# Delta rule and expert attention on one core: a shorter norm for the first two units, a folded sign, and a re-planned order of steps

## The chip, the cores and the metric

The kernel runs on one core of one Trainium2 chip. The metric is device time in microseconds (us), of which lower is better: the median of three runs, for the kernel before 444.77 us (442.21 to 446.26). One per cent is 4.4 us. Names of engines: PE is TensorE (PEld its weight loads), DVE is VectorE, ACT is ScalarE, POOL is GpSimd, SP is SyncE, which only starts transfers here.

## The reference, cut to what matters

There are 4 batches, 8 heads, 768 tokens and a head width of 48. The first part is a delta rule over time for each head; its output, heads side by side (768 x 384 for each batch), is the input of the second part, an attention in four experts of which each token uses two.

```
k_n = k / (norm(k) + 1e-6)
for t in range(768):                       # per batch and head
    y[t]  = q[t] @ state
    state = state + beta[t] * outer(k_n[t], v[t] - k_n[t] @ state)
x = y, heads side by side                  # 4 x 768 x 384
logits = x @ w_gate; topk = the 2 largest of 4; w = softmax over these 2
for e in range(4):
    a   = causal softmax(0.125 * (x @ wq[e]) @ (x @ wk[e]).T)
    out += w[e] (0 where e is not chosen) * (a @ (x @ wv[e])) @ wo[e]
```

## The kernel before, in words

The work is cut into six units of 256 tokens, numbered n = 0 to 5: units 0, 1, 2 are the three thirds of one pair of batches, units 3, 4, 5 those of the other pair. A unit has four chunks c of 64 tokens, and every chunk has 16 pairs of batch and head. Within a chunk the recurrence is solved in closed form: products of keys (`ga`), a triangular system of the tokens among themselves, and then, chunk after chunk, the state.

The kernel is one long list of steps, the string `ORDER`. Each word is a step with its arguments (and, after an @, the PSUM banks that it uses): `s0.4` is row 4 of the first unit's solve. The list is walked once from left to right and every step writes its instructions at once, so the list sets the order of the work on every engine and of the transfers on SP. Engines wait for each other by semaphores only. No planner runs inside the kernel: the numbers and the order in the string are all there is.

The steps that matter here, for a unit n:

- `lk`, `lq`, `lt`, `lv`, `lc`, `ww` load from memory (SP). `ga` multiplies keys with keys on PE; `ge.n.c.0` and `ge.n.c.1` copy the products from PSUM on ACT (line 207, into gf and into at or ax). `dx` (ACT, line 397) and `dy` (DVE, line 402) put unit 0's products into another layout, and `bi` (DVE, line 442) transposes them into the matrix `B`, in which a partition holds one small triangular system. Unit 0's B is a part of the tile vs; the others use the tile b.
- `nm` makes the norms from the diagonal of B: `aa`, which is beta over the squared (norm + 1e-6), and `nt`, the norm + 1e-6, transposed. Units 0 and 1 use square roots on ACT, whose function table has to be loaded first; units 2 to 5 use Newton steps on DVE.
- For unit 0, `bz` (POOL, line 449) clears what lies above the diagonal, `bs` (DVE, line 454) scales B's rows with minus aa, and `s0.1` to `s0.15` (DVE, lines 459, 461, 468, 469) solve the system in 14 steps and scale the columns. For the other units `sv.n.0` (DVE, line 522), `sv.n.1` to `sv.n.31` (POOL, lines 528, 530, 532) and `sv.n.32` (DVE, line 536) do the same.
- `tn` and `bo` (DVE, lines 475 and 472) transpose back. `p1`, `w1`, `p2`, `w2`, `t2` join the halves of the systems for units 0 and 1, `m1`, `we`, `m2`, `me`, `tc0`, `cl` the blocks of 32 to 64.
- Then the recurrence, chunk by chunk: `vs` (POOL, line 586: values times nt), `ks`, `xs`, `tx` (PE: the transform), `us`, `ku`, `se`, `yy`, `yc`, `yh`, `yl`, and `hx`, six transfers on SP (line 674) that turn a part of the output (tile h) into the input of the second part (tile xu).
- The second part: `pj` (PE, xu with wh and wl: queries and keys), `kh`, `kl`, `pv`, `ve`, `lg`, `gt`, `mx`, `mk`, `mr`, `sc`, `ex`, `av`, `oe`, `ft`, `fo`, `oo`, `so`. `gp` and `pm` are the products of queries with keys for the first part and their masking (DVE, line 394).
- `fl.k` and `fz.k` are fillers: k matmuls on a tile of zeros (zb, bf16), 384 and 320 columns wide, whose results nobody reads.

Line 205 is the one helper that writes all matmuls, line 207 the one that writes most ACT copies, so matmuls and copies are told apart by their tiles.

Of the kernel before, what the change touches and what calls it, by code (L numbers as in the profile page):

```python
# [33 lines left out]
s0.7 lq.0.1 s0.8 ge.1.0.1 ge.1.0.0 s0.9 ax.0.1 fl.8@4 ga.1.2@23 lt.0.2 s0.10 s0.11 s0.12 ge.1.1.1 ax.0.0 fl.6@4
gp.0.3@56 s0.13 s0.14 s0.15 ge.1.2.1 ge.1.2.0 tn.0 wh.2 gd.1 lq.1.2 bo.0 fl.18@4 p1.0.0@7 lq.1.1 p1.0.1@2 w1.0.0.0 wh.1
w1.0.0.1 hold p1.0.3@3 w1.0.1.0 wl.2 pm.0.3.0 pm.0.3.1 p2.0.0@7 ww.4 wl.1 w1.0.1.1 lv.0.3 gp.0.1@56 w2.0.0 p2.0.1@4 ww.3
t2.0.0 bi.1 m1.0.0@7 w1.0.3.0 p1.0.2@2 we.0.0 tc0.0.0 pm.0.1.0 w1.0.2.0 cl.0.0.0 tc0.0.1 vs.0.0 w2.0.1 pm.0.1.1 cl.0.0.1
t2.0.1 fl.10@7 m2.0.0@67 m1.0.1@4 w1.0.2.1 me.0.0.0 vs.0.1 me.0.0.1 w1.0.3.1 tc0.1.0 tx.0.0@56 we.0.1 vs.0.3 nm.1.0
p2.0.2@4 us.0.0.0 cl.0.1.1 us.0.0.1 nm.1.1 ku.0.0 w2.0.2 yy.0.0@23 nm.1.2 se.0.0.1 yc.0.0 tc0.1.1 p2.0.3@7 se.0.0.0
sv.1.0 yh.0.0.1 yh.0.0.0 ks.0.1@56 sv.1.1 xs.0.1 sv.1.2 w2.0.3 yl.0.0.0 fl.5@4 m2.0.1@67 cl.0.1.0 yl.0.0.1 vs.0.2  # L40
me.0.1.1 me.0.1.0 wh.3 t2.0.2 fl.4@4 tx.0.1@67 t2.0.3 us.0.1.1 nm.1.3 wl.3 tc0.2.0 us.0.1.0 tc0.2.1 fl.6@4 yy.0.1@23
ww.5 sv.1.3 m1.0.2@6 lv.1.0 m1.0.3@4 sv.1.4 yc.0.1 we.0.3 wh.4 lq.1.3 ku.0.1 cl.0.2.0 yh.0.1.1 yh.0.1.0 gp.0.2@45 sv.1.5
se.0.1.1 yl.0.1.1 yl.0.1.0 we.0.2 sv.1.6 se.0.1.0 pm.0.2.0 hx.0.0 wl.4 pm.0.2.1 cl.0.2.1 fl.10@7 m2.0.2@56 sv.1.7
# [893 lines left out]
```

## Time and profile before

| | us |
|---|---|
| median of three runs (lowest, highest) | 444.77 (442.21, 446.26) |
| the profiled execution, whole | 444.41 |
| its span, first to last instruction | 442.7 |
| PE busy in the span | 412.6 (93%) |
| fillers (L205, p<-zb) among these | 39.7 |
| DVE, ACT, POOL busy | 272.3, 207.9, 209.7 |

The profile is of one execution, whose whole time is 1.71 us longer than its span and 0.36 us below the median. Times are counted from the start of the span. A matmul row counts as busy whether its result is used or not, so 93% holds the fillers too. Mean granted clock of TensorE over the span: 0.992 of full speed.

### The profile page before, as it was taken

The page shows a single profiled execution, that of the slowest core. Times are in us where ns is not written, and L with a number is a line of the kernel's source. Part 1 is how long each engine was busy: PE and PEld are TensorE (multiplying, and loading weights), DVE is VectorE, ACT ScalarE, POOL GpSimd, SP SyncE. Part 2 cuts the span into 40 slices and gives each one's busy share as a digit, 9 for nine tenths or more (in the row PEclk, how much of TensorE's full clock was granted, in tenths as well). Part 3 has the DMA queues.
Part 4 walks back from the last instruction along what each step waited for, and adds up shares of the span by engine and source line. Part 5 has one row for each costly group of instructions (what it writes and reads, how often), then busy time and mean ns, then how long its engine had stood idle before and what let it go on. Part 6 is the DMA issues. An engine that isn't in the chain of part 4 may idle for free.

```text
span 442.7 us, 22242 instructions
## 1 busy us (share of the span) xinstructions
PE 412.6 (93%) x10008; PEld 337.9 (76%) x10008; DVE 272.3 (62%) x557; ACT 207.9 (47%) x439; POOL 209.7 (47%) x407
## 2 busy tenths in 40 slices
...
GB/s 217 271 156 5 79 127 129 19 86 32 145 61 87 122 46 18 192 97 29 84 21 45 88 127 116 98 3 53 63 89 103 39 21 23 39 36 37 4 4 71
DMA packets 52895, 34.12 MB, mean 77 GB/s; under 512 B 34944, under 2 KB 46976, under 8 KB 52800
## 3 DMA queue, kind: packets, MB, share of 16 engines
...
q8 instruction: 78, 1.28, 1.3%
q14 instruction: 17, 0.14, 0.1%
...
## 4 chain that ended last, share of the span: by engine, by line
PE 58%; POOL 15%; DVE 12%; issue 6%; ACT 4%; DMA 3%; SPq 2%; DVEq 0%; ACTq 0%
PE p L205 57%; POOL b L530 7%; POOL tm L528 7%; SPq L674 2%; DMA xu<-h 2%; DVE qp L394 2%; PE p L840 1%; DVE gf L472 1%; DMA gf<-zb 1%; ACT gf L573 1%; DVE tn L475 1%; DVE z L609 1%; DVE b L522 1%; DVE mp L766 1%; DVE rr L430 1%
## 5 line engine op out<-in xcount | busy, mean ns | idle before, releaser
L528 POOL TENSOR_TENSOR tm<-b 128x30 f32<-128x30 f32 (+14 forms) x120 | 58.1, 485 | 41.6 <-DVE b L522 20.4
L530 POOL TENSOR_TENSOR b<-b,tm 128x30 f32<-128x30 f32 (+14 forms) x120 | 62.0, 517 | 9.4
L803 ACT ACTIVATE at<-p 128x768 f32<-128x768 f32 (+1 forms) x48 | 43.8, 919 | 33.3 <-PE p L205 31.9
L207 ACT ACTIVATE z<-p 48x384 f32<-48x384 f32 (+1 forms) x68 | 32.8, 483 | 34.7 <-DVE z L609 17.0
L766 DVE TENSOR_REDUCE mp<-p 128x2 f32<-128x1024 f32 (+3 forms) x40 | 44.3, 1115 | 6.2 <-PE p L205 5.4
L205 PE MATMUL p<-vs,at 128*64 128x65 f32 x1344 | 46.1, 224 | 0.6 <-issue 0.6
L205 PE MATMUL p<-xu,wh 128*128 128x512 f32 (+1 forms) x168 | 43.7, 386 | 2.6 <-DMA xu<-h 2.0
L394 DVE TENSOR_TENSOR qp<-p,cs 64x512 f32<-64x512 f32 x48 | 33.0, 687 | 21.1 <-PE p L205 20.4
L205 PEld LDWEIGHTS p<-vs,at 128*64 128x64 f32 x1344 | 42.0, 138 | 4.7 <-issue 1.9
L205 PE MATMUL p<-zb 128*128 128x384 bf16 (+1 forms) x204 | 39.7, 333 | 1.4 <-DVE e L337 1.2
L205 PEld LDWEIGHTS p<-xu,wh 128*128 128x128 f32 x168 | 28.2, 194 | 8.7 <-issue 2.1
L205 PE MATMUL p<-qp,z 64*48 64x64 f32 (+2 forms) x1120 | 30.6, 221 | 2.2 <-issue 0.9
L205 PE MATMUL p<-qh,kh 64*128 64x128 f32 (+1 forms) x192 | 30.3, 310 | 0.9 <-ACT at L803 0.6
L205 PEld LDWEIGHTS p<-qp,z 64*48 64x48 f32 (+2 forms) x1120 | 24.7, 120 | 7.8 <-DVE z L609 2.1
L807 POOL TENSOR_SCALAR_AFFINE_SELECT at<-at 128x512 f32<-128x512 f32 x24 | 16.3, 685 | 30.0 <-ACT at L803 30.0
L205 PEld LDWEIGHTS <-zb 128*128 128x128 bf16 x204 | 18.0, 100 | 12.5 <-issue 2.3
L586 POOL TENSOR_TENSOR kv<-kv,nt 128x384 f32<-128x384 f32 x24 | 19.7, 830 | 16.0 <-DVE nt L436 10.5
L205 PE MATMUL p<-qh,kl 64*128 64x128 f32 (+1 forms) x192 | 27.1, 277 | 0.0
L205 PE MATMUL p<-wh,xu 128*128 128x260 f32 x144 | 26.7, 296 | 0.4 <-DMA xu<-h 0.2
L205 PE MATMUL p<-ql,kh 64*128 64x128 f32 (+1 forms) x192 | 27.0, 276 | 0.0
L205 PE MATMUL p<-mr,sl 64*128 64x128 f32 (+1 forms) x192 | 26.9, 275 | 0.0
L760 DVE TENSOR_TENSOR p<-p,km 128x512 f32<-128x512 f32 (+1 forms) x32 | 18.0, 564 | 11.4 <-PE p L205 10.6
...
## 6 DMA issues: line engine op xcount, KB each, us to landing
...
```

The source lines that it names most:

```text
L205: T.matmul(o, lhsT=a, rhs=b, start=start, stop=True, skip_group_check=True)
L207: copy = lambda o, a: S.activation(o, a, AF.Copy)
L394: V.tensor_tensor(turns(QP[zi(n, c) % RQ][r, f]), gv(n, c)[r], PMK[r, None, None, :].to_broadcast([64, 2, 2, 128]), op=OP.mult)
L430: V.reciprocal(r, g0)
L528: G.tensor_tensor(tv, B2[:, i:i + 1, i + 1:].to_broadcast([128, i, m]), B2[:, 0:i, i:i + 1].to_broadcast([128, i, m]), op=OP.mult)
L530: G.tensor_tensor(B2[:, 0:i, i + 1:], B2[:, 0:i, i + 1:], tv, op=OP.add)
L586: G.tensor_tensor(vt, vt, NRM[n % 2][:, c * NP:c * NP + NP, None].to_broadcast([128, NP, HD]), op=OP.mult)
L674: nc.sync.dma_start(XU[n % 2][64 * f + HD:64 * f + 64, :, i, hb].bitcast(F32), H3[r:r + 16].bitcast(F32))
L760: V.tensor_tensor(g[:, :, :, 128 * nb - 128:], g[:, :, :, 128 * nb - 128:], KM[:, None, None, :].to_broadcast([128, 2, per, 128]), op=OP.add)
L766: V.tensor_reduce(o[:, :, y0:y0 + per], g, axis=AX.X, op=OP.max, negate=True)
L803: S.activation(at(n, b, y, kp)[:, :, 0:w], two(("sc", n, b, y, kp), w), AF.Exp, scale=0.125)
L807: G.affine_select(a, a, pattern=[[0, 2], [0, 2], [1, 128]], compare_op=OP.is_ge, fill=0.0, base=0, channel_multiplier=-1)
```

## The change: the norm of units 0 and 1, the scaling of unit 0, and a new order

**The norm of units 0 and 1.** Before, `nm.n.0` took two square roots on ACT, `nm.n.1` three DVE operations to make nn = norm + 1e-6, `nm.n.2` three more for aa, and `nm.n.3` the transposition. After, `nm.n.0` is one square root (of 4e-12 times x, for x the squared norm) and `nm.n.1` three DVE operations that make aa at once, from x + 2e-6 norm + 1e-12; `nm.n.2` takes the second square root and a copy of x on ACT, and `nm.n.3` makes the norm itself by one Newton step, adds 1e-6 and transposes, five DVE operations. **The first scaling.** `bs` multiplies with plus aa in one operation in place of two with minus aa; the solve of unit 0 subtracts where it added (`half`), and a new step `na` writes minus aa on ACT into unit 1's aa tile, for use in `s0.15`.

```diff
         if n < 2:
             if k == 0:
+                S.activation(nn, BD(n), AF.Sqrt, bias=E0, scale=4e-12)
+            elif k == 1:
+                V.scalar_tensor_tensor(nn, nn, 1e-12, BD(n), op0=OP.add, op1=OP.add)
+                V.reciprocal(r, nn)
+                V.tensor_tensor(aa, r, BT[:, n], op=OP.mult)
+            elif k == 2:
                 S.activation(g0, BD(n), AF.Sqrt, bias=E0)
-                S.activation(ss, BD(n), AF.Sqrt, bias=E0, scale=0.25)
-            elif k == 1:
+                copy(ss, BD(n))
+            else:
                 V.reciprocal(r, g0)
-                V.scalar_tensor_tensor(r, r, 0.5, BD(n), op0=OP.mult, op1=OP.mult)
-                V.scalar_tensor_tensor(nn, r, 1e-6, ss, op0=OP.add, op1=OP.add)
-            elif k == 2:
-                V.tensor_tensor(r, nn, nn, op=OP.mult)
-                V.reciprocal(r, r)
-                V.tensor_tensor(aa, r, BT[:, n], op=OP.mult)
-            else:
+                V.scalar_tensor_tensor(r, r, 0.5, ss, op0=OP.mult, op1=OP.mult)
+                V.tensor_scalar(r, r, 1e-6, None, op0=OP.add)
+                V.scalar_tensor_tensor(nn, g0, 0.5, r, op0=OP.mult, op1=OP.add)
                 V.transpose(nt, nn)
...
     def bs():
-        for x in range(2):
-            a, b = NV[0]["aa"][:, None, 16 * x:16 * x + 16].to_broadcast([128, 16, 16]), BX(0)[:, x]
-            V.scalar_tensor_tensor(b, b, -1.0, a, op0=OP.mult, op1=OP.mult)
+        a, b = NV[0]["aa"].rearrange("p (x i) -> p x i", x=2), BX(0)
+        V.tensor_tensor(b, b, a[:, :, None, :].to_broadcast([128, 2, 16, 16]), op=OP.mult)
+
+    def na():
+        S.activation(NV[1]["aa"], NV[0]["aa"], AF.Copy, scale=-1.0)
...
-        E.tensor_tensor(b[:, :, 0:i, i + 1:], b[:, :, 0:i, i + 1:], tv, op=OP.add)
+        E.tensor_tensor(b[:, :, 0:i, i + 1:], b[:, :, 0:i, i + 1:], tv, op=OP.add if n else OP.subtract)
...
-            a, b = NV[0]["aa"].rearrange("p (x i) -> p x i", x=2), BX(0)
+            a, b = NV[1]["aa"].rearrange("p (x i) -> p x i", x=2), BX(0)
```

**The order.** `ORDER` is written anew from its second line on. Two lines of it, around the first norm:

```diff
-lk.1.0 nm.0.1 lt.0.3 bz ci pm.0.0.1 lq.1.0 ge.0.2.1 ge.0.0.0 nm.0.2 ge.0.2.0 ww.1 bs fz.30 ga.1.1@67 lv.0.0 ge.1.1.0
+pm.0.0.1 nm.0.0 nm.0.2 lk.1.3 nm.0.1 ax.0.1 lq.0.2 bz pm.0.0.0 fl.14@7 ga.1.2@45 bs ga.1.1@67 lv.0.2 s0.1 ww.2 ge.1.1.0
```

Fillers, counted in the string (matmuls of `fl`, `fz`): before 152 and 52, after 121 and 94. Ahead of the first `pj` they are 91 and 33 before, 61 and 52 after; from `bi.2` to the end 54 and 19 before, 55 and 42 after. After `bi.2` the larger groups of the changed kernel are fz.10 (ahead of `yy.1.0`), fl.6 (ahead of `ks.1.1`), fz.8 (ahead of `m2.1.1`), fl.9 (ahead of `tx.2.0`), fl.9 (ahead of `mx.1.0.1.0`) and fz.9 (ahead of `yy.2.1`). Up to the first `pj` the lists hold the same work of PE. At `bi.2` the changed list has five pieces of `pj` more behind it, and at `sv.3.32` one.

Three places show how the new list moves instructions. Lines of the changed kernel are shifted by -1 or by +3 against those of the kernel before.

First place, ACT before, from the last copies ahead of the first square roots: gf and at from p are the copies `ge` of unit 0, L397 is `dx.2`, wh from at is a weight copy, sl is a constant.

```order
L207 ACTIVATE gf_81<-p_63 128x512 [waits DVE_49]
L397 ACTIVATE tn<-p_63,cs 128x256 [waits PE_49]
L207 ACTIVATE at_114<-p_63 128x128
L207 ACTIVATE wh_139<-at_115 128x512 [waits DMAHW5_49]
L413 ACT_TABLE_LOAD
L413 ACTIVATE g_89<-vs,e_150 128x32 [waits DVE_49]
L414 ACTIVATE ss_88<-vs,e_150 128x32
L207 ACTIVATE sl<-at_115 128x256 [waits DMAHW6_49]
L207 ACTIVATE at_114<-p_63 128x128
L207 ACTIVATE gf_81<-p_63 128x512 x2
```

Three copies of `ge` stand behind the two roots. ACT after, the same place:

```order
L206 ACTIVATE gf_81<-p_63 128x512 [waits DVE_49]
L396 ACTIVATE tn<-p_63,cs 128x256 [waits PE_49]
L206 ACTIVATE wh_139<-at_115 128x512 [waits DMAHW5_49]
L396 ACTIVATE tn<-p_63,cs 128x256 [waits PE_49]
L206 ACTIVATE at_114<-p_63 128x128 [waits DVE_49] x2
L206 ACTIVATE gf_81<-p_63 128x512
L206 ACTIVATE at_114<-p_63 128x128
L206 ACTIVATE gf_81<-p_63 128x512 x2
L412 ACT_TABLE_LOAD
L412 ACTIVATE nn_91<-vs,e_150 128x32 [waits DVE_49]
L418 ACTIVATE g_89<-vs,e_150 128x32
L206 ACTIVATE ss_88<-vs 128x32
```

All eight of unit 0's copies now stand ahead of the table load and the first root, and of the two at copies behind `dx.2` one waits for DVE (`dy.2`).

Second place, DVE before, behind the solve of unit 0: L475 is `tn.0`, L472 `bo.0`, L486 `w1`, L394 `pm`, L498 `w2.0.0`, L501 `t2.0.0`, L442 `bi.1`.

```order
L475 STREAM_TRANSPOSE tn<-vs 128x32x32 [waits DVE_49]
L472 STREAM_TRANSPOSE gf_81<-vs 128x32x32 [waits Activation_49]
L486 TENSOR_SCALAR at_113<-p_63,cs 128x8x32 [waits Activation_49]
L394 TENSOR_TENSOR qp_74<-p_63,cs 64x512 x2
L486 TENSOR_SCALAR at_113<-p_63,cs 128x8x32 [waits Activation_49]
L498 TENSOR_TENSOR gf_81<-gf_81,p_63 128x8x32 [waits DVE_49,PE_49]
L501 STREAM_TRANSPOSE tn<-gf_81 128x256 [waits DVE_49]
L442 STREAM_TRANSPOSE b<-gf_82 128x1024 [waits DMAHW2_49,DMAHW1_49]
```

The transposition of the norm of unit 0 (L424) is long done here: before, it stands behind the first row of the solve. DVE after, the same place:

```order
L478 STREAM_TRANSPOSE tn<-vs 128x32x32 [waits DVE_49]
L393 TENSOR_TENSOR qp_74<-p_63,cs 64x512 [waits PE_49]
L393 TENSOR_TENSOR qp_74<-p_63,cs 64x512
L475 STREAM_TRANSPOSE gf_81<-vs 128x32x32 [waits Activation_49]
L489 TENSOR_SCALAR at_113<-p_63,cs 128x8x32 [waits Activation_49] x2
L393 TENSOR_TENSOR qp_72<-p_63,cs 64x512 x2
L501 TENSOR_TENSOR gf_81<-gf_81,p_63 128x8x32 [waits DVE_49,PE_49]
L489 TENSOR_SCALAR at_113<-p_63,cs 128x8x32 [waits DVE_49,Activation_49]
L504 STREAM_TRANSPOSE tn<-gf_81 128x256 [waits DVE_49]
L443 STREAM_TRANSPOSE b<-gf_82 128x1024 [waits DMAHW4_49,DMAHW3_49]
L501 TENSOR_TENSOR gf_81<-gf_81,p_63 128x8x32 [waits PE_49]
```

A pair of `pm` stands ahead of `bo.0` (L475) and another pair ahead of `w2.0.0` (L501); the five operations of `nm.0.3` follow two instructions behind the last row, so behind `bi.1` (L443).

Third place, DVE before, ahead of the scaling that starts unit 2's solve (L522, `sv.2.0`); L438 is the last operation of its norm and L698 is `kl`.

```order
L437 RECIPROCAL rr_90<-rr_90 128x32 [waits DVE_49]
L438 TENSOR_TENSOR aa_92<-rr_90,bt 128x32 [waits DVE_49]
L698 TENSOR_TENSOR kl<-p_63,kh 128x2x128 [waits Activation_49]
L698 TENSOR_TENSOR kl<-p_63,kh 128x2x128 [waits PE_49,Activation_49]
L522 SCALAR_TENSOR_TENSOR b<-b,aa_92 128x1024 [waits DVE_49]
```

DVE after, the same place, with a copy `us.1.0.0` (L612) in front:

```order
L438 RECIPROCAL rr_90<-rr_90 128x32 [waits DVE_49]
L439 TENSOR_TENSOR aa_92<-rr_90,bt 128x32 [waits DVE_49]
L612 COPY z_101<-p_63 64x384 [waits Activation_49]
L525 SCALAR_TENSOR_TENSOR b<-b,aa_92 128x1024 [waits DVE_49]
L701 TENSOR_TENSOR kl<-p_63,kh 128x2x128 [waits Activation_49] x2
```

The two `kl` have gone behind the scaling, and one copy has come ahead of it.

## Rows read from the trace of the kernel before

**Rows 1.** The page, the chain of waits: share of the span by engine.

```profile
PE 58%; POOL 15%; DVE 12%; issue 6%; ACT 4%; DMA 3%; SPq 2%; DVEq 0%; ACTq 0%
```

**Rows 2.** Windows: length, busy of PE, PEld, DVE, ACT, POOL, granted clock, DMA.

```profile
0.00:100.00 100.00, 88.96 (x2525) 70.35 (x2527) 65.36 (x156) 52.32 (x127) 35.22 (x75) 0.98 0.46 121
100.00:220.00 120.00, 110.26 (x2662) 85.98 (x2658) 74.80 (x137) 50.20 (x110) 78.37 (x149) 1.00 0.33 84
220.00:443.00 223.00, 213.40 (x4830) 181.60 (x4828) 132.18 (x266) 105.39 (x205) 96.09 (x184) 0.99 0.20 54
```

**Rows 3.** Same windows, fillers (tile zb) alone: length, PE busy first.

```profile
100.00:220.00 120.00, 13.32 (x67) 5.32 (x67) 0.00 (x0) 0.00 (x0) 1.00 0.33 84
```

**Rows 4.** Timeline of ACT, 9 to 16 us: start, length, instruction, idle before it.

```profile
9.95 0.64 ACT L207 ACTIVATE wh<-at 128x512 fp32r<-128x512 f32 x1
10.61 1.28 ACT L413 ACT_TABLE_LOAD   x1
12.59 0.35 ACT L413 ACTIVATE g<-vs,e 128x32 f32<-128x32 f32 x1 [0.69 <-DVE vs L442]
...
13.39 0.26 ACT L207 ACTIVATE at<-p 128x128 f32<-128x128 f32 x1
13.55 1.07 ACT L207 ACTIVATE gf<-p 128x512 f32<-128x512 f32 x2
```

**Rows 5.** Timeline of DVE, 9 to 17 us.

```profile
9.94 0.61 DVE L402 SCALAR_TENSOR_TENSOR tn<-p,cs,tn 128x128 f32<-128x128 f32 x2 [0.51 <-ACT tn L397]
10.58 1.97 DVE L442 STREAM_TRANSPOSE vs<-tn 128x1024 f32<-128x1024 f32 x1
...
13.31 0.35 DVE L416 RECIPROCAL rr<-g 128x32 f32<-128x32 f32 x1
...
15.47 0.19 DVE L422 TENSOR_TENSOR aa<-rr,bt 128x32 f32<-128x32 f32 x1
15.77 0.76 DVE L454 SCALAR_TENSOR_TENSOR vs<-vs,aa 128x256 f32<-128x256 f32 x2
16.57 0.19 DVE L459 TENSOR_TENSOR tm<-vs 128x28 f32<-128x28 f32 x1
```

**Rows 6.** Timeline of POOL and of ACT's next table load.

```profile
14.06 0.99 POOL L449 TENSOR_SCALAR_AFFINE_SELECT vs<-vs 128x256 f32<-128x256 f32 x2 [0.88 <-DVE rr L417]
...
54.44 1.28 ACT L343 ACT_TABLE_LOAD   x1
55.73 0.20 ACT L343 ACTIVATE rs<-zb 128x1 f32<-128x1 bf16 x1
```

**Rows 7.** Timeline of DVE and POOL, 29 to 37 us.

```profile
29.61 1.39 DVE L394 TENSOR_TENSOR qp<-p,cs 64x512 f32<-64x512 f32 x2
...
32.19 1.92 DVE L442 STREAM_TRANSPOSE b<-gf 128x1024 f32<-128x1024 f32 x1
...
35.66 0.83 POOL L586 TENSOR_TENSOR kv<-kv,nt 128x384 f32<-128x384 f32 x1
```

**Rows 8.** Timeline of PE: fillers, `tx.0.0`, first `pj`; of SP: `hx.0.0`.

```profile
10.74 4.25 PE L205 MATMUL p<-zb 128*128 128x320 bf16 x30
...
24.33 3.10 PE L205 MATMUL p<-zb 128*128 128x384 bf16 x18
...
37.42 0.68 PE L205 MATMUL p<-kv,gf 64*64 64x48 f32 x32 [0.67 <-ACT gf L573]
...
51.13 5.00 SPq L674 DMA_DIRECT2D xu<-h  x6
...
56.83 0.54 PE L205 MATMUL p<-xu,wh 128*128 128x256 f32 x2 [1.58 <-DMA xu<-h]
```

**Rows 9.** Timeline of DVE, 100 to 103 us.

```profile
100.48 0.76 DVE L698 TENSOR_TENSOR kl<-p,kh 128x256 fp32r<-128x256 f32 x2
101.16 1.22 DVE L522 SCALAR_TENSOR_TENSOR b<-b,aa 128x1024 f32<-128x1024 f32 x1
```

**Rows 10.** Window of 3 us behind the first `pj`; granted clock third from last.

```profile
58.00:61.00 3.00, 3.00 (x43) 2.69 (x42) 0.42 (x1) 0.53 (x2) 1.92 (x3) 0.50 0.64 206
```

More of the change, by code (lines that the diff above doesn't have):

```diff
@@ L34 @@
[L34 to L43, printed above, removed]
@@ new lines @@
+lk.3.1 pv.1.1.1@7 kh.1.3.2 sv.2.27 kl.1.3.2 pj.1.2.2.0@3 sv.2.28 pj.1.2.2.1 sv.2.29 pj.1.2.2.2 sv.2.30 pj.1.0.2.0@6
+sv.2.31 kh.1.2.2 pj.1.1.2.0@4 ve.1.1.1 kl.1.2.2 pj.1.0.2.1 sv.2.32 pj.1.1.2.1 sc.0.0.1.0@23 lg.1.1.1 bo.2 pj.1.0.2.2
+pj.1.1.2.2 tn.2 to.2 kh.1.0.2 pv.1.1.0@5 ex.0.0.1.0@1 m1.2.0@7 lg.1.1.0 sm.0.0.1 kl.1.0.2 ve.1.1.0 kh.1.1.2 vs.2.3
+ga.3.2@56 kl.1.1.2 m1.2.1@2 sm.0.0.0 ge.3.2.1 ga.3.1@34 ge.3.2.0 gt.1.0 vs.2.1 ga.3.3@56 ge.3.1.0 ge.3.3.0 gt.1.1
+ge.3.3.1 ge.3.1.1 we.2.0 fz.5 ga.3.0@45 sm.0.1.0 gp.2.2@67 ge.3.0.0 vs.2.2 av.0.0.0.0@3 gt.1.2 ge.3.0.1 gd.3 sm.0.1.1
@@ new lines @@
+mr.1.0.1.0 sv.3.5 us.2.1.0 sv.3.6 mr.1.0.1.1 fz.9 yy.2.1@23 mx.1.0.0.0@67 sv.3.7 yc.2.1 mk.1.0.0.0 mr.1.0.0.0 ku.2.1
+yh.2.1.0 fo.0.0.1@5 sv.3.8 yh.2.1.1 se.2.1.1 yl.2.1.1 yl.2.1.0 se.2.1.0 sv.3.9 ks.2.2@23 oo.0.0.1 so.0.0.1 ft.0.1@5
+xs.2.2 mt.1.0@4 sv.3.10 so.0.0.0 m2.2.1@67 mo.1.0 lk.4.3 oh.0.1 sc.1.0.1.0@23 lv.3.1 me.2.1.0 ol.0.1 sv.3.11 hx.2.0
+me.2.1.1 mx.1.1.0.1@45 ex.1.0.1.0@2 fo.0.1.1@6 mk.1.1.0.1 sv.3.12 mr.1.1.0.1 mx.1.1.1.1@23 oo.0.1.1 sv.3.13
+sc.1.0.1.1@45 mk.1.1.1.1 lq.3.3 mr.1.1.1.1 sc.1.0.0.0@67 ex.1.0.1.1@4 sv.3.14 lk.4.1 mx.1.1.0.0@23 so.0.1.1 tx.2.2@45
```

257 lines of the change are left out of this document (128 added, 129 removed).

## The prediction

> **What bounds the kernel now.** I read the chain of waits first: of the span, 58% lies on PE, 15% on POOL, 12% on DVE, 6% is issue, 4% ACT and 3% transfers [rows 1]. The share of PE is not one limit: the table of three stretches tells where PE is the bound. From 220 us to the end PE is busy 213.40 of 223 us [rows 2] and hardly any filler is left, so there the time is PE's work and only work removed or done earlier shortens it. Between 100 and 220 us PE is busy 110.26 of 120 us [rows 2], but 13.32 of these are fillers [rows 3]: 120 - 110.26 + 13.32 = 23.1 us in which PE had nothing useful to do, while unit 2's and unit 3's solves run on POOL. Before 100 us PE is 88.96 busy [rows 2], and the chain runs through the first norm, unit 0's solve on DVE, the joining, the first chunks and the transfers `hx.0.0` up to the first `pj`, for which PE waits 1.58 us [rows 8]. So the end moves by what the first `pj`, then `sv.2.0` and `sv.3.0`, move, and by useful work that goes into the 23.1 us. Of each part I ask what it does to the next of these points.
>
> **Part 1: the first norm, to the first row of the solve (before: 16.57 us [rows 5]).** On DVE the change takes a chain of six 32-wide operations between root and aa, two with a reciprocal, to three with one. In the rows a reciprocal takes 0.35 and a small one 0.19, with gaps up to the 0.11 between 15.66 and 15.77 [rows 5]. With some 0.05 for a gap, six are 2 x 0.40 + 4 x 0.25 = 1.8 and three are 0.40 + 2 x 0.25 = 0.9, so 0.9 less. `bs` is one operation over the same elements in place of two; I take its 0.76 as unchanged [rows 5], since no row has it in one piece. One root in place of two ahead of the norm saves 0.25 more or so (the first root ends at 12.94, the reciprocal starts at 13.31 [rows 4, 5], and the second root lies between). All this counts if the root comes as early. It does not. Before, the table load starts at 10.61, behind a weight copy, and is through at 11.89, 0.69 ahead of the root, which waits for `bi.0` (DVE, 10.58 to 12.55) [rows 4, 5]: the load is hidden by a transposition. After, eight copies stand ahead of the load, and one of them waits for `dy.2`, which ends at 10.55 [rows 5]. Then come five copies. Three of this kind (at, gf, gf) take 13.39 to 14.62, 1.23 us [rows 4]; five, of which three gf and two at, about 2.0. So the load goes from 12.55 to 13.83 and the root starts at 13.85 in place of 12.59: +1.26. If the copies begin a little earlier and half of them are done when `dy.2` ends, it is +0.5; if they begin with a later wait, +1.6. Sum: -0.9 - 0.25 + 1.26 = +0.1. POOL's `bz` (0.99 [rows 6]) has to be through ahead of `bs` too; it now waits for the copy of the diagonal on ACT, which follows the second root, some 0.7 behind the first: 13.85 + 0.7 + 0.99 = 15.5, still ahead of the `bs` at about 15.8. Behind the roots on ACT stand unit 1's copies, which `bi.1` wants at 32.19 only [rows 7], and `na`, which `s0.15` wants at the solve's end: both cost nothing while the solve of some 8 us covers them. **Term 1: 0.0** (first row of the solve at 16.6), from -1.0 (load still hidden) to +0.5.
>
> The Trainium skill, "ScalarE: Activation LUTs", section "What ACT_TABLE_LOAD costs", counts beside the load's 1.28 us a drain of about 1.38 us for each switch. The later load shows no such pause: it starts at 54.44, and the next operation at 55.73, 1.29 us after [rows 6]. By the page the root would start about 1.4 us later and the total below would be 444.4; I go by the rows.
>
> **Part 2: from the solve's end to the first `pj` (before 56.83 [rows 8]).** Two steps move onto the path. A pair of `pm` (1.39 [rows 7]) goes ahead of `bo.0`, so `p2.0.0`, `w2.0.0` and `m1.0.0` are some 1.0 to 1.7 later. And the norm's second half (five operations, about 0.35 + 4 x 0.2 and gaps, 1.25) goes behind `bi.1`, whose end moves from 34.11 to about 36; so `vs.0.0` on POOL, 0.83 long and before started at 35.66 [rows 7], ends near 39.0, and `tx.0.0`, which needs it, starts near 39.3 in place of 37.42 [rows 8]: +1.9. What gives it back: behind `tx.0.0` the old list has fillers of 5, 4, 6 and 10 ahead of the next PE steps and `tx.0.1`, `m2` and `yy` wait behind them; the new one puts `m1.0.1`, `m2.0.1` and `m1.0.2` ahead of the chunks and has groups of 3, 1, 5 and 3 there. At 0.163 us each ((3.10 - 0.33) / 17 [rows 8]) the 13 fewer are about 2 us. The two steps of the chain that then set the first `pj`, `tx.0.1` and `yy.0.1`, come out near where they were, and behind them the same six transfers run, which SP issues from 51.13 to 56.13 [rows 8]. **Term 2: -0.1** (first `pj` at 56.7), from -2.0 (the moved work all used) to +1.9 (nothing given back).
>
> **Part 3: first `pj` to `sv.2.0` (before 101.16 [rows 9]).** PE's work is the same but for five pieces of `pj` that now come earlier. The `kl` pair ahead of `sv.2.0` goes behind it. It took 0.68 of the path, from 100.48 to 101.16 [rows 9]; the copy `us.1.0.0` that comes ahead instead was inside the norm before and is neutral. POOL's solve of unit 2 starts as much earlier. **Term 3: -0.7**, from -2.0 (if the early `pj` also leave waits out) to +1.0.
>
> **Part 4: to `sv.3.0` and the end.** The solve of unit 2 on POOL is the same chain. Between `bi.3` and `sv.3.0` DVE gets other operations between those of the norm, and the key products come in another order: -0.3, from -3 to +3. Behind 220 us PE is the bound; one `pj` of work is done ahead at `sv.3.32`, some 0.5 to 0.75 us: -0.3 as the end of the list is the same chain. Fillers grow by 11 in the sum; most stand where PE waits anyway. **Term 4: -0.6.**
>
> **Sum.** 0.0 - 0.1 - 0.7 - 0.6 = -1.4 from the profiled 444.41: **443.0 us**. The profiled execution was 0.36 below the median of 444.77, so against that median it is 0.4% less. I take within 1% (4.4 us) to be what a measurement of this kernel can't tell from no change, as its three runs spread over 4.05 us.
>
> **Rivals.**
> *A, faster: the new order uses PE's empty time.* Of the 23.1 us between 100 and 220 us, the five `pj` pieces and the `pj`, `mx` and `sc` that move across `sv` rows can fill some. If a third is used, 23.1 / 3 = 7.7 go from the profiled 444.41: 437. In favour: the gaps exist, and a half clock may go with a wait: in the 3 us behind the wait at the first `pj` the granted clock is 0.50, 1.2 of 2.4 GHz, with PE busy all the time [rows 10], which costs 1.5 us. Against: the lists' work at `sv.3.32` differs by one `pj` only, and that is what can be won behind 220. Chance 0.28.
> *B, slower: fillers stand in front of ready work.* From `bi.2` on they grow from 54 and 19 to 55 and 42: one of 0.163 and 23 of 0.14 (4.25 / 30 [rows 8]), 3.4 us more; the six large groups (24 of fl, 27 of fz) are 24 x 0.163 + 27 x 0.14 = 7.7 us and stand on the chunk chain of units 1 and 2, each ahead of a matmul whose operand DVE or ACT makes. A group costs what it still runs when that operand is there. If two thirds of the 7.7 us do, that is +5 on 444.4: 449.5. It decides from about 4.5 us, somewhat over half. Against: the groups may be sized to the wait. Chance 0.17.
> *C, the load stays hidden.* If the copies are through before `bi.0`, Part 1 gives -1.0 and the first `pj` follows if `hx.0.0` does: -1.0 - 1.4: 442. Chance 0.05, for `dy.2` ends only as `bi.0` begins [rows 5].
> Forecast 0.50.
>
> **How the numbers follow.** The forecast's own range is 440.5 to 446 by the terms' ends taken together. To leave out no more than 2 in 10 the range must take in most of A and B: 436 to 449.5. Faster by over 1% (below 440.3): all of A and a little of the forecast, 0.30. Slower (over 449.2): B and a little, 0.18. Within 1%: 0.52.
>
> **What the profile after will show.** ACT: a table load that starts at 12 us or later, the first root near 13.85; first row of the solve on DVE near 16.6. If the root is at 12.6, Part 1 is wrong and C holds. `tx.0.0` near 39.3 and the first `xu,wh` matmul near 56.7: past 58.5 Part 2 fails, before 55 it gave back too much. `sv.2.0` near 100.4 with `kl` behind it, and `sv.3.0` about 1 us earlier than before. If it is more than 4 us earlier, rival A; if over 3 us later, with filler groups that end behind their operand, rival B. The idle time plus fillers of PE between 100 and 220 us should stay near 23; a fall by a third is A. From `sv.3.0` to the end the time should be as before within 1 us; if a difference arises there, I have missed a mechanism.

## The result, and the profile after

| | kernel before | changed kernel |
|---|---|---|
| median, us (lowest to highest, executions) | 444.39 (442.08 to 451.64, 20) | 448.88 (443.70 to 488.27, 20) |
| ratio, 95% interval | | 1.007 (1.0041 to 1.0100) |
| profiled execution, us | 444.41 | 445.52 |
| its span, us; mean granted clock | 442.7; 0.992 | 443.8; 0.976 |

The changed kernel is slower by 0.7%. I had forecast 443.0, a little faster: the sign is wrong. That the median lies in the range is due to the range's width and not to the mechanism. The ratios here and below leave out executions over 1.5% slower than the fastest of their kernel and so need not be the ratio of the medians, which count all.

The page of the changed kernel, busy time and chain of waits by engine:

```profile
PE 414.9 (93%) x10019; PEld 341.6 (77%) x10019; DVE 271.3 (61%) x558; ACT 206.3 (46%) x442; POOL 209.7 (47%) x407
...
PE 52%; DVE 16%; POOL 15%; issue 5%; ACT 5%; DMA 3%; SPq 3%; DVEq 0%; ACTq 0%; POOLq 0%
```

The busy shares hardly tell the two kernels apart; of the chain PE has 6 points less and DVE 4 more than before [rows 1]. The windows tell more. The same three stretches of the changed kernel (length, busy of PE, PEld, DVE, ACT and POOL, granted clock, DMA share, GB/s):

```profile
0.00:100.00 100.00, 90.54 (x2411) 71.64 (x2412) 63.00 (x145) 51.22 (x129) 34.78 (x74) 0.91 0.45 121
100.00:220.00 120.00, 109.66 (x2769) 86.56 (x2768) 76.16 (x147) 51.26 (x110) 78.96 (x149) 1.00 0.32 81
220.00:443.00 223.00, 214.75 (x4843) 183.44 (x4841) 132.15 (x268) 103.85 (x205) 95.99 (x184) 0.99 0.20 55
```

Beside [rows 2] one number stands out: the granted clock of the first 100 us is 0.91, where it was 0.98. PE is busier there (90.54 for 88.96 us) and has done less: 2411 matmuls for 2525. A narrower window of the changed kernel, 28 to 47 us, shows where:

```profile
28.00:47.00 19.00, 19.00 (x430) 15.40 (x430) 13.48 (x27) 7.87 (x21) 4.73 (x6) 0.55 0.28 83
```

and the same window of the kernel before:

```profile
28.00:47.00 19.00, 16.92 (x585) 13.99 (x583) 14.85 (x31) 9.84 (x26) 7.50 (x14) 1.00 0.18 54
```

PE is busy 19.00 of 19 us and finishes 430 matmuls; before it finished 585 in 16.92 us. From 30 to 47 us the clock stands at 0.50, 1.2 of 2.4 GHz. What lies ahead of that is in the timeline of PE (and of SP, last line):

```profile
21.40 4.38 PE L204 MATMUL p<-zb 128*128 128x320 bf16 x31
27.30 4.77 PE L204 MATMUL p<-tn,at 64*64 64x32 f32 x128 [1.51 <-DVE tn L478]
43.32 1.11 PE L204 MATMUL p<-kv,gf 64*64 64x48 f32 x32
60.76 0.38 PE L204 MATMUL p<-xu,wh 128*128 128x256 f32 x1 [0.81 <-DMA xu<-h]
55.89 4.64 SPq L677 DMA_DIRECT2D xu<-h  x6
```

The long filler group fz.31 starts at 21.40, ends at 25.78, and PE waits 1.51 us for `tn.0`, up to 27.30. Before, the group ahead of `p1` started at 24.33 and ended with the wait [rows 8]. `tx.0.0` starts at 43.32 in place of 37.42, the transfers `hx.0.0` go out from 55.89 in place of 51.13, and the first `pj` starts at 60.76 in place of 56.83 [rows 8].

The first norm came out close to the forecast. ACT and DVE of the changed kernel, 9 to 17 us:

```profile
10.41 0.28 ACT L206 ACTIVATE at<-p 128x128 f32<-128x128 f32 x1 [0.51 <-DVE tn L401]
11.22 1.11 ACT L206 ACTIVATE gf<-p 128x512 f32<-128x512 f32 x2
12.34 1.28 ACT L412 ACT_TABLE_LOAD   x1
13.64 0.35 ACT L412 ACTIVATE nn<-vs,e 128x32 f32<-128x32 f32 x1
...
16.45 0.19 DVE L462 TENSOR_TENSOR tm<-vs 128x28 f32<-128x28 f32 x1
```

A copy waits for DVE up to 10.41, the load comes at 12.34, the root at 13.64 (13.85 forecast), the first row of the solve at 16.45 (16.6 forecast, 16.57 before [rows 5]). The copies ahead of the load end at 12.33, and from the load's start to the next operation it is 1.30 us. The drain of some 1.38 us that the Trainium skill gives for each switch ("ScalarE: Activation LUTs", section "What ACT_TABLE_LOAD costs") isn't there; the trace does not agree with it here either.

Behind the first `pj` this execution of the changed kernel wins back more than I had summed. DVE, the start of unit 2's solve and the `kl` that now stand behind it, the start of unit 3's solve, and the same of the kernel before:

```profile
104.10 1.23 DVE L525 SCALAR_TENSOR_TENSOR b<-b,aa 128x1024 f32<-128x1024 f32 x1
105.36 0.76 DVE L701 TENSOR_TENSOR kl<-p,kh 128x256 fp32r<-128x256 f32 x2
...
166.56 1.22 DVE L525 SCALAR_TENSOR_TENSOR b<-b,aa 128x1024 f32<-128x1024 f32 x1
...
163.42 1.23 DVE L522 SCALAR_TENSOR_TENSOR b<-b,aa 128x1024 f32<-128x1024 f32 x1
```

Measured against the kernel before, the first `pj` is 3.93 us late, `sv.2.0` 2.94 (104.10 for 101.16 [rows 9]), `sv.3.0` 3.14 (166.56 for 163.42), the end of the span 1.1. From the first `pj` to the end this execution is 2.8 us quicker; I had summed 1.3. One pair of executions can't tell whether that is the change.

### The profile page after: what moved, and what is told of

Same layout as the page of the kernel before. It is cut to its first block, busy times and chain, and to the rows that moved or that the text cites. A ratio compares the mean times of both kernels' runs of the same rounds, so it can differ in the third digit from the quotient of the medians.

```text
span 443.8 us, 22250 instructions
## 1 busy us (share of the span) xinstructions
PE 414.9 (93%) x10019; PEld 341.6 (77%) x10019; DVE 271.3 (61%) x558; ACT 206.3 (46%) x442; POOL 209.7 (47%) x407
## 4 chain that ended last, share of the span: by engine, by line
PE 52%; DVE 16%; POOL 15%; issue 5%; ACT 5%; DMA 3%; SPq 3%; DVEq 0%; ACTq 0%; POOLq 0%
PE p L204 50%; POOL b L533 7%; POOL tm L531 7%; SPq L677 2%; DMA xu<-h 2%; DVE tn L478 2%; DVE gf L475 2%; DVE b L443 1%; DVE qp L393 1%; PE p L843 1%; ACT gf L206 1%; DMA gf<-gf 1%; ACT z L206 1%; DVE z L612 1%; ACT at L806 1%
## 5 line engine op out<-in xcount | busy, mean ns | idle before, releaser
L204 PE MATMUL p<-vs,at 128*64 128x65 f32 x1344 | 44.0, 223 | 0.7 <-DVE qp L393 0.2
L204 PE MATMUL p<-zb 128*128 128x384 bf16 (+1 forms) x215 | 42.6, 337 | 1.4 <-DVE e L336 1.2
L204 PEld LDWEIGHTS p<-vs,at 128*64 128x64 f32 x1344 | 41.1, 137 | 3.1 <-DVE qp L393 0.8
L810 POOL TENSOR_SCALAR_AFFINE_SELECT at<-at 128x512 f32<-128x512 f32 x24 | 15.2, 640 | 39.0 <-ACT at L806 38.8
L204 PEld LDWEIGHTS <-zb 128*128 128x128 bf16 x215 | 19.5, 102 | 12.3 <-issue 2.4
L598 DVE TENSOR_TENSOR x<-kv,p 128x384 f32<-128x384 f32 x22 | 12.2, 553 | 18.5 <-PE p L204 15.6
```

What stands on the lines that cost most here:

```text
L204: T.matmul(o, lhsT=a, rhs=b, start=start, stop=True, skip_group_check=True)
L598: V.tensor_tensor(split(X), split(KV[zi(n, c) % RV][:, 1]), duo(("ks", n, c), HD), op=OP.subtract)
L810: G.affine_select(a, a, pattern=[[0, 2], [0, 2], [1, 128]], compare_op=OP.is_ge, fill=0.0, base=0, channel_multiplier=-1)
```

## The experiments

Theory W: PE's wait ahead of `p1` is followed by half clock, and that is the loss. Theory O: the order on DVE (`pm` ahead of `bo.0`, the norm's second half behind `bi.1`) makes the chain late, and the clock is a by-product. Each run is compared with the kernel before on the same chip.

| run | ratio to before (95%) | median, us (before there) |
|---|---|---|
| e1_fill_wait | 1.0013 (0.9964 to 1.0063) | 446.16 (446.03) |
| e2_before_wait | 1.0103 (1.0002 to 1.0204) | 456.07 (446.03) |
| e3_norm_only | 1.0109 (1.0062 to 1.0155) | 447.55 (446.03) |
| e4_norm_cover | 1.0026 (0.9984 to 1.0068) | 446.36 (446.26) |
| e5_thick | 1.0074 (1.0023 to 1.0125) | 449.13 (446.03) |
| e6_both_waits | 0.9947 (0.9896 to 0.9997) | 447.60 (446.26) |
| e7_before_pj | 1.0003 (0.9957 to 1.0050) | 444.87 (446.26) |
| e8_after_again | one execution | 449.63 |
| e9_six_groups_out | 1.0158 (1.0082 to 1.0233) | 451.91 (446.03) |
| e10_both_again | 0.9960 (0.9910 to 1.0011) | 446.84 (446.03) |
| e11_before_both | 1.0063 (1.0028 to 1.0097) | 446.33 (444.43) |
| e12_old_norm | 1.0055 (1.0015 to 1.0095) | 447.23 (444.43) |

Below about 1% the ratio and the medians can part: e3 is 1.1% slower by its ratio and 0.3% by the medians, e6 0.5% faster by the one and 0.3% slower by the other. So what a run tells below that size is read from its trace, or is left open.

**e1: the wait ahead of p1 filled.**

```diff
-hold fz.31 p1.0.1@2
+hold fz.41 p1.0.1@2
```

> The changed kernel with the filler group ahead of p1.0.1 ten matmuls longer (fz.41 for fz.31), so that PE is busy until about 27.2 us and its wait of 1.51 us ahead of the first p1 matmul (27.30) shrinks to about 0.1. Theory W (that wait is what the half clock from 30 to 47 us follows from, and the half clock is the loss): granted clock 1.00 from 28 to 48 us, first xu,wh matmul at 56.5 to 57.7 in place of 60.76, ratio to the kernel before 0.992 to 1.000. Theory O (the order on DVE, pm ahead of bo.0 and the norm's second half behind bi.1, makes the chain late; the clock is a by-product): first xu,wh matmul at 59 or later, ratio about 1.007 as for the changed kernel.

Windows of e1 (30 to 47 and 58 to 65 us), then its PE at `p1` and at the first `pj`:

```profile
30.00:47.00 17.00, 14.98 (x557) 12.23 (x557) 12.80 (x27) 11.57 (x30) 7.01 (x13) 1.00 0.33 93
58.00:65.00 7.00, 6.96 (x126) 5.80 (x127) 1.18 (x7) 1.69 (x5) 6.08 (x15) 0.52 0.33 106
...
28.49 0.71 PE L204 MATMUL p<-tn,at 64*64 64x32 f32 x18
57.89 1.12 PE L204 MATMUL p<-xu,wh 128*128 128x256 f32 x2 [1.46 <-DMA xu<-h]
```

The clock is full from 30 to 47 us. `p1` starts 1.2 us later than in the changed kernel (28.49 for 27.30; PE waited 1.26 us for issue near 22 us, so the longer group overran), and still the first `pj` is 2.9 us earlier, 57.89 for 60.76. That is theory W's decisive row: later into the stretch, earlier out of it. The first `pj` is 0.2 over the bound I had given and the ratio just past its upper end; in this profile a second wait, 1.46 us ahead of that `pj`, is followed by half clock, from 58 to 65 us.

**e2: the same wait made in the order before.**

```diff
-bo.0 fl.18@4 p1.0.0@7
+bo.0 fl.9@4 p1.0.0@7
```

> The kernel before with the filler group ahead of its first p1 halved (fl.9 for fl.18), so that PE waits about 1.5 us there (25.9 to 27.4). Nothing else is changed. Theory W: half clock follows from about 28 to 30 us on, for 4 to 17 us, the first xu,wh matmul comes 1 to 4 us after 56.83, ratio 1.002 to 1.010. Theory O, or if the later filler groups of the order before keep the clock up by themselves: granted clock stays 1.00 there, first xu,wh at 56.8, ratio 1.000.

PE of e2 at `p1`, and its window from 30 to 47 us:

```profile
27.12 2.14 PE L205 MATMUL p<-tn,at 64*64 64x32 f32 x61 [1.44 <-DVE tn L475]
...
30.00:47.00 17.00, 15.57 (x397) 12.93 (x395) 9.82 (x21) 6.09 (x17) 3.98 (x7) 0.64 0.09 27
```

There are nine matmuls on zeros less, and half clock follows from 28 to 42 us; the first `pj` comes at 61.56, 4.7 us after 56.83 [rows 8]. It is 1.0% slower by the ratio, 2.3% by the medians, and the profiled execution is the slowest of the six (457.17 us): theory W, at the upper edge of its range or beyond it. DVE's order is that of before, so theory O can't say this.

**e3: the new arithmetic alone, in the order before.** The functions are the changed kernel's; in the list only the norm's steps move (in unit 1 `nm.1.2` goes behind `nm.1.0`), and `na` comes in.

```diff
-bi.0 lk.1.3 pm.0.0.0 nm.0.0 lk.1.0 nm.0.1 ... nm.0.2 ge.0.2.0 ... s0.1 lv.0.2 nm.0.3 s0.2 ... t2.0.0 bi.1 m1.0.0@7
+bi.0 lk.1.3 pm.0.0.0 nm.0.0 nm.0.2 lk.1.0 nm.0.1 ... ge.0.2.0 ... s0.1 lv.0.2 s0.2 ... sq0 na ... t2.0.0 bi.1 nm.0.3 m1.0.0@7
```

> The order before with the new arithmetic alone: one root ahead of aa, the first scaling in one operation, na; the norm's second half stands behind bi.1, the roots where they were before. The table load stays hidden behind bi.0, so the first row of the solve should start about 1.0 us earlier, at 15.5 (Term 1's far end). The filler group fl.18 ends by its own length at 27.4, so p1 gains nothing or little; tx.0.0 about 38 (37.42 before). Both theories expect a ratio of 0.997 to 1.001; that the arithmetic is the slow part would show as 1.004 or more.

e3: first row of the solve (DVE), PE at `m2.0.0` and at the first `pj`:

```profile
15.55 0.19 DVE L463 TENSOR_TENSOR tm<-vs 128x28 f32<-128x28 f32 x1
37.50 0.22 PE L205 MATMUL p<-at,tn 32*32 32x32 f32 x2 [1.18 <-DVE qp L394]
60.36 0.54 PE L205 MATMUL p<-xu,wh 128*128 128x256 f32 x2 [1.49 <-DMA xu<-h]
```

The first row of the solve is 1.02 us earlier, as expected (15.5). The ratio is not: 1.011. The norm's second half, five operations, stands on DVE ahead of a `pm` that PE waits for, 1.18 us; half clock follows from 40 to 48 us, again behind the wait at the first `pj`, and from 95 to 102 us behind a wait of 1.67 us that no other engine ends.

**e4: the same with that wait filled.**

```diff
-fl.10@7 m2.0.0@67
+fl.17@7 m2.0.0@67
```

> The order before with the new arithmetic alone, as in the run that did only this, and its filler group ahead of m2.0.0 longer by seven (fl.17 for fl.10, 1.14 us), so that the wait of 1.18 us for DVE there (37.50) is covered. Theory W: clock 1.00 from 38 to 48 us, first xu,wh matmul at 57 to 58.5 in place of 60.36, ratio 1.000 to 1.005 in place of 1.011. Rival (the new arithmetic is slow by itself, through the five operations of the norm's second half on DVE): ratio stays at 1.008 or more.

PE of e4 at `tx.0.0` and at the first `pj`:

```profile
38.51 0.68 PE L205 MATMUL p<-kv,gf 64*64 64x48 f32 x32 [0.70 <-ACT gf L577]
58.09 0.39 PE L205 MATMUL p<-xu,wh 128*128 128x256 f32 x1 [1.20 <-DMA xu<-h]
```

The clock is full from 38 to 48 us, and the first `pj` comes at 58.09, 2.3 us earlier than in e3, for seven matmuls on zeros. The ratio is 1.0026 for 1.0109; the two are from two chips and their intervals overlap, and by the medians it is 0.0% for 0.3%. So the arithmetic is not shown to be the slow part; how much of e3's loss the seven matmuls undo isn't settled.

**e5: more fillers behind the wait, the wait kept.**

```diff
-fl.3@2 p2.0.1@3 ... fl.3@4 m2.0.0@67 ... fl.2@3 tx.0.0@45 ... fl.3@3 m2.0.1@56
+fl.10@2 p2.0.1@3 ... fl.10@4 m2.0.0@67 ... fl.5@3 tx.0.0@45 ... fl.6@3 m2.0.1@56
```

> The changed kernel, its wait ahead of p1 kept, with four of its thin filler groups behind it made longer (3, 3, 2, 3 to 10, 10, 5, 6: 20 more matmuls, 3.3 us at full clock). Theory W: the half clock still begins near 30 us; the fillers then cost up to double and the first xu,wh matmul comes at 61 to 66; ratio over 1.007. Rival T (the half clock comes from too little work between 28 and 47, not from the wait): clock 1.00, or back by about 40 us, first xu,wh at 57 to 59, ratio 1.000 or below.

Window of e5:

```profile
30.00:47.00 17.00, 17.00 (x373) 12.75 (x372) 10.41 (x24) 7.07 (x20) 4.73 (x6) 0.75 0.33 92
```

Half clock begins at 28 us all the same, behind a wait of 1.50, and ends at 39 in place of 47. The first `pj` is at 62.55, the ratio as without them. One sign of rival T came, the clock back by about 40 us; its others did not (no half clock, the first `pj` at 57 to 59, a ratio of 1.000). What stands behind the wait is no substitute for filling it: in this profile the fillers shortened the half clock and cost what they won.

**e6 and e10: both waits filled in the changed kernel.** The same kernel twice, on two chips.

```diff
-hold fz.31 p1.0.1@2
+hold fz.40 p1.0.1@2
...
-lk.2.1 pj.0.2.0.0@7
+lk.2.1 fz.10 pj.0.2.0.0@7
```

> The changed kernel with both waits of PE covered by zeros: fz.40 for fz.31 ahead of p1.0.1, and fz.10 (1.4 us) ahead of the first pj, where PE waited 1.46 us for the transfers in the run with the first wait covered. Theory W (each wait of about 1.5 us is followed by half clock, and that is the loss): clock 1.00 from 28 to 66 us, first xu,wh matmul still at 56.5 to 58, sv.2.0 at 101 to 102.5 in place of 104.1; ratio 0.990 to 0.998, about my forecast of 443.0. Rival (the order itself is slower): sv.2.0 at 104 and a ratio of 1.001 or more even with the clock at full.

> The changed kernel with both early waits covered (fz.40 and fz.10), once more with more executions, beside the kernel before. Theory W: ratio 0.992 to 0.999 again, first xu,wh matmul at 56 to 58 with full clock to 66 us. If it is 1.000 or more, the first measurement of this kernel was luck and the new order gains nothing even with the clock kept.

e6: PE at `p1` and at the first `pj`, DVE at `sv.2.0`, and the window from 30 to 47 us:

```profile
26.94 1.26 PE L204 MATMUL p<-tn,at 64*64 64x32 f32 x37 [0.32 <-DVE tn L478]
56.64 1.55 PE L204 MATMUL p<-xu,wh 128*128 128x256 f32 x9
99.99 1.23 DVE L525 SCALAR_TENSOR_TENSOR b<-b,aa 128x1024 f32<-128x1024 f32 x1
...
30.00:47.00 17.00, 14.77 (x527) 11.57 (x523) 12.74 (x28) 10.68 (x29) 8.03 (x15) 1.00 0.35 94
```

The clock is full up to 148 us; the first `pj` is at 56.64 (56.7 forecast), `sv.2.0` at 99.99 (100.4 forecast, 101 to 102.5 expected of this run; 101.16 before), the span 440.8 against 442.7. In e10 they are 56.74, 100.53 and 444.1, with three stretches of half clock behind 147 us. The ratios, 0.9947 and 0.9960, are 1.1% to 1.2% under the changed kernel's 1.007; by the medians these two are 0.3% and 0.2% above the kernel before, the changed kernel 1.0%. So covering both waits takes most or all of the loss away. That this version beats the kernel before is not shown: one interval ends below 1, the other at 1.0011, and by the medians of all executions it is not faster (447.60 for 446.26, 446.84 for 446.03).

**e7: the wait at the first pj filled in the order before.**

```diff
-pj.0.1.0.0@7 sv.1.10
+fz.11 pj.0.1.0.0@7 sv.1.10
```

> The kernel before with fz.11 ahead of its first pj, where PE waited 1.58 us for the transfers and half clock followed from 58 to 61 us. Theory W: clock 1.00 there, first xu,wh unchanged at 56.8, ratio 0.994 to 1.000. Rival (the half clock follows from the work behind, not from the wait): half clock at 58 to 61 all the same, ratio 1.000 or a little above.

PE of the kernel before near 22 us; then e7, PE's group ahead of `p1`, `p1` itself, and the two windows:

```profile
22.35 0.34 PE L205 MATMUL p<-kf 48*64 48x64 f32 x5 [1.10 <-issue]
...
22.73 3.10 PE L205 MATMUL p<-zb 128*128 128x384 bf16 x18
27.38 0.83 PE L205 MATMUL p<-tn,at 64*64 64x32 f32 x22 [1.55 <-DVE tn L475]
...
30.00:47.00 17.00, 15.37 (x518) 12.22 (x514) 13.06 (x30) 8.65 (x23) 7.41 (x14) 1.00 0.13 34
58.00:65.00 7.00, 6.78 (x267) 5.80 (x268) 2.81 (x6) 4.09 (x11) 5.23 (x11) 1.00 0.50 157
```

The half clock behind the first `pj` [rows 10] is gone, as theory W has it. But the rows ahead of them speak against its simple form: in this execution, without the wait for issue near 22 us, the group ended at 25.83, PE waited 1.55 us ahead of `p1` too, and no half clock followed. The first `pj` is at 56.37, `sv.2.0` at 100.12. The ratio is 1.0003 (0.9957 to 1.0050): no gain is shown.

**e8: the changed kernel once more.**

> The changed kernel once more, unchanged, for a second profile. In the first, PE had no wait for issue between 16 and 26 us, so that fz.31 ran from 21.40 to 25.78; in three other profiles it has one of 1.1 to 1.26 us near 22 us. Theory W: if such a wait is there this time, fz.31 ends near 27, p1 follows without a wait and the clock stays 1.00 to 47 us, first xu,wh near 57; if it is not there, the same half clock from 28 to 30 us on and first xu,wh at 60 to 62.

PE of e8 at `p1`, and its window:

```profile
27.12 1.09 PE L204 MATMUL p<-tn,at 64*64 64x32 f32 x31 [1.51 <-DVE tn L478]
...
30.00:47.00 17.00, 17.00 (x367) 13.40 (x369) 11.26 (x26) 7.01 (x20) 4.73 (x6) 0.51 0.32 92
```

There is no wait for issue near 22 us, fz.31 runs from 21.22 on, and there follow the same wait of 1.51, half clock from 29 to 46 us and the first `pj` at 61.77, as expected for that case.

**e9: rival B. The six larger groups behind bi.2 taken out of e6's kernel.**

```diff
-us.1.0.0 fz.10 yy.1.0@45 ... fl.6@6 ks.1.1@45 ... fz.8 m2.1.1@45 ... fl.9@2 tx.2.0@67 ... fl.9@4 mx.1.0.1.0@23 ... fz.9 yy.2.1@23
+us.1.0.0 yy.1.0@45 ... ks.1.1@45 ... m2.1.1@45 ... tx.2.0@67 ... mx.1.0.1.0@23 ... yy.2.1@23
```

> The same kernel without the six larger filler groups behind bi.2 (ahead of yy.1.0, ks.1.1, m2.1.1, tx.2.0, mx.1.0.1.0 and yy.2.1: 24 of fl, 27 of fz, about 7.7 us). Theory W: PE then waits 1 to 1.6 us at some of these places, half clock follows in one or more of them between 100 and 180 us, and the ratio to the kernel before is 0.002 to 0.010 above that of the run with the groups. Rival B (the groups stand in front of ready matmuls): sv.2.0 to sv.4.0 shorter by 2 to 5 us, ratio 0.005 to 0.010 below it.

e9: PE where fz.10 stood, and the window behind it:

```profile
100.17 2.13 PE L204 MATMUL p<-qp,z 128*48 128x64 f32 x48 [2.73 <-DVE z L612]
...
100.00:113.00 13.00, 10.41 (x299) 9.10 (x300) 8.49 (x15) 4.34 (x10) 9.83 (x23) 0.50 0.01 3
```

and the same window with the groups, in e10:

```profile
100.00:113.00 13.00, 11.08 (x372) 8.08 (x376) 9.55 (x17) 4.91 (x11) 9.52 (x22) 1.00 0.03 7
```

Half clock stands from 100 to 113 and from 168 to 178 us, and the ratio is 1.0158, 0.020 above e10 beside it (1.1% by the medians, from six executions). From `sv.2.0` to `sv.4.0` it takes 133.6 us (100.14 to 233.78), 125.3 in e10 (100.53 to 225.85); rival B had it shorter by 2 to 5. So rival B falls for these six groups: taking out their 7.7 us of zeros costs 5 to 9 us more than it saves, which is up to twice what I had put as theory W's end.

**e11: the same two covers in the order before.**

```diff
-bo.0 fl.18@4 p1.0.0@7 ... pj.0.1.0.0@7
+bo.0 fl.27@4 p1.0.0@7 ... fz.11 pj.0.1.0.0@7
```

> The kernel before with both its early waits covered: fz.11 ahead of its first pj and fl.27 for fl.18 ahead of p1 (in one profile of the order before PE waited 1.55 us there). This tells whether the new order is worth anything beside the covering. If my sum holds (new order and arithmetic -1.4 us with the clock kept), this kernel stays 0.3% or so above the changed kernel with both waits covered: ratio 0.997 to 1.000. If covering is all, the ratio is the same as there, 0.994 to 0.996.

PE of e11, the group of `fz.30`, the group ahead of `p1`, `p1`, and the first `pj`:

```profile
10.69 5.92 PE L205 MATMUL p<-zb 128*128 128x320 bf16 x30
...
24.34 4.56 PE L205 MATMUL p<-zb 128*128 128x384 bf16 x27
28.83 1.36 PE L205 MATMUL p<-tn,at 64*64 64x32 f32 x40
...
57.03 1.65 PE L205 MATMUL p<-xu,wh 128*128 128x256 f32 x9
```

Neither expectation holds: 1.0063. The nine extra matmuls run from 27.4 to 28.8, where in the kernel before `p1` started at 27.40. The cover is itself a delay of 1.4 us when PE comes to it late, as here, where half clock from 11 to 14 us had made the group of `fz.30` 5.92 us long in place of 4.25 [rows 8]. But that delay is not what the 0.6% is: of it 0.2 us are left at the first `pj` (57.03 for 56.83 [rows 8]), and `sv.2.0` comes 0.25 earlier than before (100.91 for 101.16 [rows 9]). Then `sv.3.0` is 2.0 late (165.41 for 163.42), behind both covers; why isn't shown. By the ratios e11 is 1.0% to 1.2% above e6 and e10, by the medians 0.1% to 0.3%, so whether covering is all that these have stays open.

**e12: the old arithmetic in the new order, both waits covered.** The functions of before, `nm.0.2` behind `nm.0.1`, the like for unit 1, no `na`, and fz.48 for fz.40.

```diff
-nm.0.0 nm.0.2 lk.1.3 nm.0.1 ax.0.1 ... s0.5 na ww.1 ... hold fz.40
+nm.0.0 lk.1.3 nm.0.1 nm.0.2 ax.0.1 ... s0.5 ww.1 ... hold fz.48
```

> The changed kernel with both waits covered, but with the old arithmetic in the new order: two roots and six operations ahead of aa, the first scaling in two operations, the sign as before, fz.48 for fz.40 so that the later p1 is covered as well. By Term 1 the new arithmetic is worth 0.9 + 0.25 us there: first row of the solve at 17.3 to 17.8 in place of 16.1 to 16.5, first xu,wh matmul about 1 us later than with the new arithmetic (57.3 to 58), ratio 0.002 to 0.003 higher. If the arithmetic doesn't reach the end, the ratio is the same, 0.995 to 0.996.

e12, DVE at the first row of the solve, PE at `p1` and at the first `pj`:

```profile
17.27 0.19 DVE L458 TENSOR_TENSOR tm<-vs 128x28 f32<-128x28 f32 x1
28.89 3.92 PE L204 MATMUL p<-tn,at 64*64 64x32 f32 x128
58.22 0.39 PE L204 MATMUL p<-xu,wh 128*128 128x256 f32 x1
```

The solve starts 1.56 us later than in e10 (15.71), the first `pj` 1.48 (58.22 for 56.74), `sv.2.0` 1.30 (101.83 for 100.53): a later solve does reach the path when the clock is kept. How much of this is the arithmetic is not shown: `tn.0` is through at 27.95, and `p1` waits for fz.48 up to 28.89, 0.9 us longer. The ratio is 1.0055, 0.010 above e6 and e10, three times what 1.3 us is; the profile has half clock from 149 to 156 us, longer than e10's, so the rest isn't the arithmetic alone either.

## Why the prediction was wrong

- **Part 1 held.** Five copies from `dy.2` on, the load at 12.34 (12.55), the root 1.05 later than before (1.26), the first row of the solve at 16.45 (16.6). With the load left hidden (e3) it is 15.55, the far end that I had given. That it hit so closely is in part luck: in the six other profiles of the same list (e1, e5, e6, e8, e9, e10) the first row is at 15.54 to 16.55.
- **Part 2 is the step that failed**, by a term that it put at nothing without a reason. It adds up two steps of DVE and 13 fillers fewer behind `tx.0.0`, and it has neither PE's wait ahead of `p1` nor the clock behind that wait. I did not lay PE's work ahead of `p1` beside the solve's end: fz.31 is through at 25.78, and `tn.0` frees `p1` at 27.30. The wait of 1.51 us is followed by 17 us at half clock, and the first `pj` is at +3.93 in place of -0.1, past my own bound of 58.5. e1 undoes it (2.9 us back though `p1` is later), e2 makes it in the kernel before.
- **What Part 2 did add up** was about right: in e6, with the clock kept, `tx.0.0` is at 38.62, +1.2 for my +1.9, and the first `pj` at 56.64 for my 56.7.
- **The wait is not the new list's alone.** In the profile of the kernel before PE came to `p1` without a wait, and it had waited 1.10 us for issue near 22 us. In e7, the same list up to there without that earlier wait, its group ends at 25.83, as late as fz.31 in the changed kernel, and PE waits 1.55 us. What differs is what came behind it: half clock in all three profiles of the changed list that have the wait (after, e5, e8) and in e2, none in e7. Why is open.
- **Parts 3 and 4 are not shown.** From the first `pj` to `sv.2.0` the changed kernel wins 0.99 (0.7), but the kernel before has half clock in that stretch, at 58 us; against e11, which has none there, it wins 0.5. From `sv.3.0` to the end it wins 2.0, and I had called anything over 1 us there a missed mechanism; but e6 and e10, one kernel, differ by 2.8 us in that stretch, so one pair of profiles can't tell. The points of six profiles, us:

| profile | first `pj` | `sv.2.0` | `sv.3.0` | end of span |
|---|---|---|---|---|
| before | 56.83 | 101.16 | 163.42 | 442.7 |
| e7 (before, wait at `pj` covered) | 56.37 | 100.12 | 163.62 | 441.7 |
| e11 (before, both covered) | 57.03 | 100.91 | 165.41 | 443.7 |
| after | 60.76 | 104.10 | 166.56 | 443.8 |
| e6 (changed, both covered) | 56.64 | 99.99 | 163.63 | 440.8 |
| e10 (the same) | 56.74 | 100.53 | 164.17 | 444.1 |

Where no half clock stands behind the two early waits, the old list (e7, e11) and the new one (e6, e10) overlap at every one of these points. The 1.4 us that I had summed for the change can't be seen there.

- **Rival A** had no sign: between 100 and 220 us PE's idle time and fillers are 26.8 us (120 - 109.66 + 16.43) and not less than 23. It named the half clock behind a wait, and only as something to win. The row for it [rows 10] stood in my own list; read in the other direction, that a new wait of that length would cost several us, it gives the loss. **Rival B** had the right sign, and `sv.3.0` is 3.14 us late, over the 3 that I had given for it; but 3.93 were lost ahead of the first `pj`, where its groups don't stand, and e9 speaks against it. **Rival C** was right to be small.
- **The forecast's own range**, 440.5 to 446, is not the terms' ends taken together, as I wrote: these add up to some 436 to 450.5.

The spread fits: of the 20 executions of the changed kernel three have a mean clock of 0.988 or more, and these are the three fastest, 443.70, 443.83 and 445.44 us. My 443.0 is near what the changed kernel takes when the clock stays up; its median is what it takes when it does not. What decides between them, from one execution to the next, isn't shown. The profiled execution ends only 1.1 us later than that of the kernel before; the rest of the 4.5 us between the medians lies in executions without a profile. That it has the same cause rests on the runs: with the wait ahead of `p1` filled (e1) or both waits (e6, e10), the medians are 0.0% to 0.3% above the kernel before and not 1.0%.
